# One matrix product out of eight, moved ahead of a group of attention scores in a fused attention and expert kernel

## The chip, the cores and the metric

The kernel runs on one core of one Trainium2 chip. The metric is the time of one execution on the device, in microseconds (us); a run's figure is the median of several executions. A profiled execution gives the trace of all engines of the core: TensorE (PE for its products, PEld for its weight loads), VectorE (DVE), ScalarE (ACT), GpSimd (POOL) and SyncE (SP, which here only issues DMAs).

## The reference

The inputs are q, k and v of 4 batches x 8 heads x 768 positions x 64, and three random block numbers for each of the 24 blocks of 32 positions. Attention is full matrix work under a block mask; its output, laid side by side over the heads, is the input x (3072 tokens x 512) of one expert layer with a softmax-weighted unit, a normalisation without a bias and a second product.

```
scores = (q @ k.T) / sqrt(64);  scores = where(mask, scores, -1e9)
x = softmax(scores) @ v                      # heads side by side: 3072 x 512
h = x @ w_in                                 # 3072 x 1024
solu = h * softmax(h)
ln = (solu - mean(solu)) / sqrt(var(solu) + 1e-6) * g_ln
out = ln @ w_out                             # 3072 x 512
```

## The kernel before, in words

**Tiling.** The 3072 tokens are worked in 12 passes of 256 tokens (three passes to a batch), and each pass in 12 units, so there are 144 units. A unit is one pair of heads (four pairs to a pass) and one third of the keys (256 of 768). For a unit, `scores` (L407) runs four products of 128 x 256 on TensorE into a tile of the scores' pool; `exps` (L423) takes the exponential of the whole tile (128 x 1024) on ScalarE; `outs` (L431) runs eight small products with the values (128 x 65). The mask is part of the scores' product: 24 extra rows of the keys and queries carry it. After the third unit of a pair of heads, `normalise` (L451) divides by the sums on VectorE and writes xb. The scores' pool has two buffers of two banks, so the scores of unit s + 2 need the buffer that the exponential of unit s reads.

**The layer.** When the four pairs of a pass are done, SP issues a transposing DMA of xb to xT (`x_turn`, L467). The layer then handles the pass's two tiles of 128 tokens, one after the other, while the next passes' attention goes on. For a tile, `h_mms` (L482) runs eight products of 128 x 512 into the one buffer for h; `e_exp` (L491) takes the exponential of h on ScalarE; `solu` (L499) multiplies h and e on VectorE; `ln_turn` (L510) has SP issue a transposing DMA of that product to lnT; `stats` and `rstd` (L516 and L524) work out the scale on VectorE and GpSimd; `o_mms` (L542) runs eight products of 128 x 512, one for each 128 of the 1024 columns, into the one buffer for o; `scaled` (L550) multiplies o by the scale on VectorE, and `store` (L560) has SP write the rows out.

**The order.** All this is issued from one written plan: `at(when, fn, ...)` (L290) puts a call on a list with a time in units, and `emit` (L293) calls the list sorted by that time. The order on each engine is thus the order of those numbers, and an engine waits only where an operand or a buffer isn't ready. In the loop at L773 unit s has its exponential at s (a little less at the end of a pass), the scores of unit s + 2 at s + 0.8, and its products with the values at s + 0.82 (s + 1.81 for the first unit of a pair). The function `layer` (L815) puts one tile's calls on the plan, from a list of times for pieces of h, a time for the exponential, and a list of times for pieces of o; the loop at L831 to L844 calls it for the two tiles of passes 0 to 9, 20 tiles in all, six units apart. The times of o are os + 0.84 and os + 1.83, where os is 14 units behind the tile's start (12 for the second tile of pass 9). The last two passes' tiles are planned by hand behind it and have nothing to do with the change.

**Around the change.** Between os + 0.84 and os + 1.83 stands one call for TensorE: the scores of unit os + 3, at os + 1.8 (in the second tile of pass 9 the products with the values of two units as well). Behind os + 1.83 come, at os + 1.9, the first two products of h of a later tile, and at os + 2.8 the scores of unit os + 4.

Of the kernel before, what the change touches and what calls it, by code (L numbers as in the profile page):

```python
# [208 lines left out]
def kernel(  # L209
# [25 lines left out]
    KF = d_ff // 128  # L235
# [12 lines left out]
    SLOTS = NP * UP  # L248
# [41 lines left out]
    def at(when, fn, *args):  # L290
        plan.append((when, len(plan), fn, args))
# [103 lines left out]
    def unit(s):  # L395
        ps, r = divmod(s, SLOTS)
        pr, u = divmod(r, UP)
        b, j = divmod(ps, NPB)
        return ps, b, j, pr, u
# [174 lines left out]
    with tc.manual_schedule():  # L574
# [198 lines left out]
        for s in range(n_units):  # L773
            ps, b, j, pr, u = unit(s)
# [37 lines left out]
                at(t0 + t_s, shift, b, pr, key, PC if pr == NP - 1 else 0)  # L812


        def layer(ps, i, hs, es, os):  # L815
            for when, n0, n1 in hs:
                at(when, h_mms, ps, i, n0, n1)
            at(es, e_exp, ps, i)
            head = ps == 0 and i == 0
            at(es + (0.33 if head else 0.5), solu, ps, i)  # L820
            at(es + 0.55, ln_turn, ps, i)
            at(es + (6.6 if head else 3.4 if ps == 0 else 2.45 if i == 0 else 1.7), stats, ps, i)
            at(es + (6.7 if head else 3.5), rstd, ps, i)
            for when, n0, n1 in os:
                at(when, o_mms, ps, i, n0, n1)
            out_at = 29.87 if head else os[-1][0] + 0.1
            at(out_at, scaled, ps, i, nc.vector)
            at(out_at + (2.2 if i == PC - 1 and ps < NPASS - 3 else 0.02), store, ps, i)

        LP = NPASS - 1  # L830
        for ps in range(LP):  # L831
            b0 = SLOTS * (ps + 1)
            if ps == 0:
                at(b0 + 2.4, x_first, ps)
            else:
                at(b0 - 0.1, x_turn, ps, 0, KD)
            if ps == LP - 1:
                break
            for i in range(PC):
                hs = b0 + 6 * i  # L840
                os = hs + (12 if ps == LP - 2 and i == PC - 1 else 14)
                layer(ps, i,
                      [(hs + 3.9, 0, 2), (hs + 4.85, 2, 3), (hs + 5.86, 3, 5), (hs + 6.85, 5, 7),
                       (hs + (7.79 if hs == SLOTS else 7.85), 7, 8)], hs + 8.5, [(os + 0.84, 0, 7), (os + 1.83, 7, 8)])  # L844


        ps, b0 = LP - 1, SLOTS * LP
# [176 lines left out]
```

## Time and profile before

| what | us |
|---|---|
| median of 3 runs | 208.02 (207.55 to 208.16) |
| the profiled execution | 208.32 |
| its span, first to last instruction | 206.8 |
| granted clock of TensorE over the span | 1.0 |

A line of the timeline has the start in us from the span's start, the length in us, the engine, the line of the kernel, the operation, what it writes and reads, and how many instructions are merged into the line; the bracket tells for how long the engine had been idle and who ended that. The products of TensorE are pipelined: the record of one is longer than the distance to the next, so distances between starts tell what a product costs. A few records of products are missing from the trace, which shows as x6 where seven were issued and as a short gap. In the chain of work each piece is start, length, what; it is followed back from the last instruction, at each step to what released it.

### The profile page before, as it was taken

To read this page: it belongs to the slowest core of one execution; us is meant where nothing else is said; L and a number is where in the kernel's file an instruction comes from. 1 tells how busy PE (TensorE), PEld (TensorE's weight loads), DVE (VectorE), ACT (ScalarE), POOL (GpSimd) and SP (SyncE) were. 2 spreads that over 40 slices of the span, in tenths; PEclk is the share of its full clock that TensorE was granted. 3 is DMA by queue.
4 is the path that set the end of the run, shared out by engine and by line. 5 is a ranking of instruction groups with operands and counts; after the bars stand their busy time and mean duration, and the time that the engine had idled before them with its cause. 6 is when DMAs were issued, how large, how long until landed. Compare 5 with 4: busy or idle time off the path is not lost.

```text
span 206.8 us, 5603 instructions
## 1 busy us (share of the span) xinstructions
PE 199.0 (96%) x2204; PEld 138.8 (67%) x2238; DVE 141.1 (68%) x331; ACT 175.2 (85%) x209; POOL 110.2 (53%) x167
## 2 busy tenths in 40 slices
PE   7999999999999999999999999999999999999992
PEld 2679967676676676676676676676676676667451
DVE  5688888988755765765665666655665656677982
ACT  6799979889889889889889889879889889897471
POOL 7966799696868274478286273559281110111120
PEclk9999999999999999999999999999999999999999
DMA  5999999979999879999999889999872484556314
GB/s 158 334 367 229 361 373 271 229 134 248 235 264 346 203 168 335 212 153 220 175 232 294 204 161 338 166 241 193 166 196 51 101 105 50 107 125 111 59 50 162
DMA packets 73906, 42.02 MB, mean 203 GB/s; under 512 B 55828, under 2 KB 69396, under 8 KB 73876
## 3 DMA queue, kind: packets, MB, share of 16 engines
q1 hardware_dynamic: 72932, 40.06, 84.1%
q0 software_dynamic: 528, 1.05, 2.7%
q10 hardware_dynamic: 416, 0.52, 0.8%
q8 instruction: 18, 0.29, 0.6%
q14 instruction: 12, 0.10, 0.1%
HBM read 23.07 MB, written 6.29 MB: 142 GB/s over the span
## 4 chain that ended last, share of the span: by engine, by line
PE 90%; DMA 4%; DVE 3%; issue 1%; DVEq 0%
PE sco L416 30%; PE op L444 18%; PE o L547 17%; PE h L487 16%; DMA xT<-xb 3%; PE warm_t L403 2%; DMA lnT<-solu 1%; PE tp_k L346 1%; PE oe L547 1%; PE mean_ps L753 1%; PE tp_q L356 1%; PE he L873 1%; DVE KT L371 1%; DVE QT L664 1%; PE ln_tp L883 0%
## 5 line engine op out<-in xcount | busy, mean ns | idle before, releaser
L427 ACT ACTIVATE exs<-sco 128x1024 bf16<-128x1024 f32 x144 | 141.0, 1024 | 10.3 <-PE sco L416 7.7
L416 PE MATMUL sco<-QT,KT 88*128 88x256 bf16 x576 | 87.4, 274 | 0.3
L416 PEld LDWEIGHTS <-KT 88*128 88x128 bf16 x576 | 54.8, 98 | 31.6 <-issue 4.7
L444 PE MATMUL op<-VA,exs 128*128 128x65 bf16 x1152 | 51.8, 194 | 0.5
L444 PEld LDWEIGHTS <-exs 128*128 128x128 bf16 x1152 | 48.5, 97 | 3.7 <-DVE xb L458 0.3
L487 PE MATMUL h<-w_in_sb,xT 128*128 128x512 bf16 x153 | 48.7, 378 | 0.7
L547 PE MATMUL o<-w_cen_sb,lnT 128*128 128x512 bf16 x166 | 43.3, 379 | 1.0 <-DMA lnT<-solu 0.4
L540 POOL TENSOR_TENSOR rstd<-vpe,mhalf 128x1 f32<-128x1 f32 x24 | 13.2, 549 | 45.4 <-DVE vpe L538 38.9
L457 DVE RECIPROCAL recip_all<-op 128x4 f32<-128x4 f32 x48 | 8.7, 181 | 39.7 <-PE op L444 39.5
L327 POOL COPY KT<-pd 64x768 bf16<-64x768 bf16 (+2 forms) x30 | 21.2, 706 | 23.9 <-DMA pd<-nat 22.8
L496 ACT ACTIVATE e<-h 128x1024 bf16<-128x1024 f32 x22 | 22.5, 1023 | 10.7 <-PE h L487 10.6
L522 DVE BATCH_NORM_STATS2 stats<-solu 128x6 f32<-128x512 bf16 x48 | 30.6, 680 | 0.1
L508 DVE TENSOR_TENSOR solu<-h,e 128x1024 bf16<-128x1024 f32 x22 | 26.7, 1215 | 1.5 <-ACT e L496 1.5
L547 PEld LDWEIGHTS <-lnT 128*128 128x128 bf16 x176 | 15.8, 98 | 14.2 <-DMA lnT<-solu 0.9
L558 DVE TENSOR_SCALAR ot<-o,rstd 128x512 f32<-128x512 f32 x20 | 15.0, 751 | 10.8 <-issue 8.2
L327 POOL COPY QT<-pd 64x768 bf16<-64x768 bf16 (+2 forms) x30 | 20.8, 694 | 1.5
L458 DVE TENSOR_TENSOR xb<-op,recip_all 128x256 bf16<-128x256 f32 x48 | 20.4, 424 | 1.7
L327 POOL CAST nat<-st_q 128x768 bf16<-128x768 f32 (+2 forms) x19 | 13.6, 713 | 14.3 <-DMA st_q<-in_q_dram 14.3
L487 PEld LDWEIGHTS <-xT 128*128 128x128 bf16 x176 | 16.1, 98 | 4.7 <-DMA xT<-xb 0.8
L327 POOL CAST VA<-st_v 128x768 bf16<-128x768 f32 x16 | 13.4, 847 | 1.4 <-DMA st_v<-in_v_dram 0.9
L327 POOL CAST nat<-st_k 128x768 bf16<-128x768 f32 x15 | 12.4, 826 | 3.3 <-DMA st_k<-in_k_dram 3.1
L538 DVE TENSOR_TENSOR vpe<-es,mv 128x1 f32<-128x1 f32 x24 | 6.7, 278 | 0.9
(89 smaller groups left out, 116.5 us busy)
## 6 DMA issues: line engine op xcount, KB each, us to landing
st_v<-in_v_dram SPq DMA_DIRECT2D x16, 384.0 KB, 5.9
out_dram<-ot SPq DMA_DIRECT2D x23, 256.0 KB, 2.8
st_k<-in_k_dram SPq DMA_DIRECT2D x15, 384.0 KB, 5.8
st_q<-in_q_dram SPq DMA_DIRECT2D x12, 384.0 KB, 7.9
w_out_f<-in_moe_w_out_dram SPq DMA_DIRECT2D x4, 512.0 KB, 7.4
st_q<-in_q_dram SPq DMA_DIRECT2D x4, 256.0 KB, 7.9
w_in_sb<-in_moe_w_in_dram POOLq DMA_DIRECT2D x1, 1024.0 KB, 12.0
st_q<-in_q_dram SPq DMA_DIRECT2D x4, 128.0 KB, 4.4
```

The source lines that it names most:

```text
L327: eng.tensor_copy(out=o, in_=i)
L416: nc.tensor.matmul(sco[:, hh, kk * QW : (kk + 1) * QW], KT[b % 2][0:KR, h * NCH + 2 * u + kk, :], QT[b % 2][0:KR, h * NCH + PC * j : h * N ...
L427: nc.scalar.activation(out=exs_of[ps, pr][:, u].rearrange("p a b c -> p (a b c)"), in_=sco_of.pop(s).rearrange("p a b -> p (a b)"), func=A ...
L444: nc.tensor.matmul(op[:, hh, ic, :], exs[:, u, hh, kk, ic * TQ : (ic + 1) * TQ], VA[b % 2][:, 2 * pr + hh, 2 * u + kk, :], start=(u == 0 a ...
L458: nc.vector.tensor_tensor(out=xb_of[ps][:, pr].rearrange("p c (h d) -> p h c d", h=2), in0=op[:, :, :, 0:D], in1=recip.broadcast_to([TQ, 2 ...
L487: nc.tensor.matmul(h_of[ps, i][:, half, :], xT_of[ps][:, c * PC + i, :], w_in_sb[:, c, half * HF : (half + 1) * HF], start=(c == 0), stop= ...
L496: nc.scalar.activation(out=o, in_=h, func=ACT.Exp, scale=1.0, accum_out=esum_all[:, t : t + 1])
L508: nc.vector.tensor_mul(out=so, in0=h, in1=e)
L522: nc.vector.bn_stats(out=stat_of[ps, i][:, half, :], in_=so[:, half, :])
L540: nc.gpsimd.tensor_tensor(out=rstd_of[ps, i], in0=vpe, in1=mhalf, op=ALU.pow)
L547: nc.tensor.matmul(ops_of[ps, i], lnT_of[ps, i][:, c, :], w_cen_sb[:, c, :], start=(c == 0), stop=(c == KF - 1), skip_group_check=True)
L558: nc.vector.tensor_scalar(out=o, in0=i_, scalar1=r, scalar2=None, op0=ALU.mult)
```

## The change

The function `layer` takes one time for o in place of a list of pieces. All eight products of o are issued at os + 0.84, so the eighth is no longer behind the scores of unit os + 3 but ahead of them. The scaling keeps its time: it was 0.1 behind the last piece (os + 1.83 + 0.1), and is now os + 0.84 + 1.09. On the queues of the other four engines the order of the instructions stays the same; on TensorE one weight load and one product change places with four weight loads and four products in 20 places (and in one of these 20 with 16 more of each, the products with the values).

```
-        def layer(ps, i, hs, es, os):
+        def layer(ps, i, hs, es, o_at):
...
-            for when, n0, n1 in os:
-                at(when, o_mms, ps, i, n0, n1)
-            out_at = 29.87 if head else os[-1][0] + 0.1
+            at(o_at, o_mms, ps, i, 0, KF)
+            out_at = 29.87 if head else o_at + 1.09
             at(out_at, scaled, ps, i, nc.vector)
...
-                       (hs + (7.79 if hs == SLOTS else 7.85), 7, 8)], hs + 8.5, [(os + 0.84, 0, 7), (os + 1.83, 7, 8)])
+                       (hs + (7.79 if hs == SLOTS else 7.85), 7, 8)], hs + 8.5, os + 0.84)
```

## The prediction, made before the changed kernel was run

> **What bounds the kernel now.** I read the page first (busy shares, the chain that ended last), then the chain of work in windows, then the timeline of one tile's round, then the waits of the queues.
>
> ```profile
> span 206.8 us, 5603 instructions
> ...
> PE 199.0 (96%) x2204; PEld 138.8 (67%) x2238; DVE 141.1 (68%) x331; ACT 175.2 (85%) x209; POOL 110.2 (53%) x167
> ...
> PE 90%; DMA 4%; DVE 3%; issue 1%; DVEq 0%
> ```
>
> TensorE carries 90% of the chain; ScalarE is next with 85% busy. A reordering on TensorE adds and removes no work, so it can only pay by filling a stall inside that 90%. To find one I look in the chain for a group that takes longer in one place than in another. This is the chain in three windows; columns are start, length, what.
>
> ```profile
> 41.27 0.44 PE sco L416 x4
> ...
> 48.87 0.51 PE sco L416 x4
> ...
> 109.00 1.51 PE o L547 x7
> 110.51 0.51 PE sco L416 x4
> 111.02 0.22 PE o L547
> 111.24 0.43 PE h L487 x2
> 111.67 0.44 PE sco L416 x4
> ...
> 180.19 0.51 PE sco L416 x4
> ...
> 186.22 0.44 PE sco L416 x4
> ```
>
> Four score products take 0.44 us, but 0.51 us where they follow the seven products of o: 0.07 us of nothing. The change has 20 such places, one for each token tile of passes 0 to 9. From 48.87 (first) to 180.19 (last) 17 of them show it. The other three do not: the ones at 41.27 and 186.22, and the one at 133.7, where TensorE had been held up just before. The timeline of the round at 110 us says what the scores wait for (columns: start, length, engine; narrow windows, so that ScalarE's exponentials stand one by one).
>
> ```profile
> 108.34 1.02 ACT L496 ACTIVATE e<-h 128x1024 bf16<-128x1024 f32 x1 [0.57 <-PE h L487]
> 108.84 1.67 PE L547 MATMUL o<-w_cen_sb,lnT 128*128 128x512 bf16 x7
> 109.36 1.02 ACT L427 ACTIVATE exs<-sco 128x1024 bf16<-128x1024 f32 x1
> 109.59 1.22 DVE L508 TENSOR_TENSOR solu<-h,e 128x1024 bf16<-128x1024 f32 x1
> 110.26 1.02 ACT L427 ACTIVATE exs<-sco 128x1024 bf16<-128x1024 f32 x1
> 110.42 0.60 PE L416 MATMUL sco<-QT,KT 88*128 88x256 bf16 x4
> 110.42 0.31 PEld L416 LDWEIGHTS <-KT 88*128 88x128 bf16 x3 [0.20 <-issue]
> 110.75 0.10 PEld L547 LDWEIGHTS <-lnT 128*128 128x128 bf16 x1
> 110.86 0.31 PEld L487 LDWEIGHTS <-xT 128*128 128x128 bf16 x2
> 111.08 0.59 PE L487 MATMUL h<-w_in_sb,xT 128*128 128x512 bf16 x2
> 111.16 2.06 ACT L427 ACTIVATE exs<-sco 128x1024 bf16<-128x1024 f32 x2
> 111.51 0.60 PE L416 MATMUL sco<-QT,KT 88*128 88x256 bf16 x4
> 112.92 0.60 PE L416 MATMUL sco<-QT,KT 88*128 88x256 bf16 x4
> 113.56 1.02 ACT L427 ACTIVATE exs<-sco 128x1024 bf16<-128x1024 f32 x1 [0.33 <-PE sco L416]
> ```
>
> Seven products from 108.84 at 1.51/7 = 0.216 us each are through at 110.35, but the scores start at 110.42. There are two score buffers, so these scores (unit os+3, os being the plan's slot of the o products) need the one that the exponential of unit os+1 reads. That one ran from 109.36 to 110.38, and 0.04 us later the scores start. It was late because ScalarE first had to do e, which in turn had waited 0.57 us for h. So once a round the path runs through ScalarE for 0.07 to 0.08 us.
>
> **The change part by part.** The plan moves one weight load and one product of o, 20 times, ahead of the scores of os+3 and on TensorE alone. The order of the instructions on the other four queues is the same, DMA issues included; no wait is added. The written times of the scaling and the store are also the same (os + 1.93 both ways).
>
> *The moved product.* It takes 0.216 us wherever it stands. Eight end at 108.84 + 8 x 0.216 = 110.57, after the buffer is free at 110.42, so the scores no longer wait; they start 0.15 later than now. They take 0.43, then h starts at 111.00 instead of 111.08. **Gain 0.07 (chain) to 0.08 (starts) a round; I take 0.075**, and 17 x 0.075 = 1.28 us if nothing else is late next.
>
> *What is late next, one by one.* (a) The first h product needs VectorE's product of h and e (one h buffer), done at 109.59 + 1.22 = 110.81; its weight load now starts at 110.86. A weight load starts here as the product ahead of it starts (110.75 is 0.33 behind the scores' 110.42), so in the new order it is due at 110.57 + 0.33 = 110.90: 0.04 to spare. (b) The scores of os+4 come at 111.43 and need the exponential that ends at 110.26 + 1.02 = 111.28, plus 0.04: 0.11 to spare. (c) The exponential of os+3 can start 0.64 behind its scores (112.92 to 113.56, where ScalarE stood waiting), so at 111.21 instead of 111.16; if it loses its overlap with the one ahead (spacing 0.90 against a length of 1.02) it starts at 111.28, 0.12 late. ScalarE has 0.33 of idle two exponentials later in this round and 0.57 ahead of e in the other kind of round, so this is taken up. (d) VectorE's scaling of o can start half a microsecond sooner; it is queued behind the product of h and e and holds up nobody. (e) The store of it is issued by SP, which hardly waits for that scaling:
>
> ```profile
> SPq L563 <- DVE ot L558: 0.2, 1, 0.2
> ```
>
> so no transfer moves because of it.
>
> *Where the gain cannot be kept.* The 17 gains pile up only if what TensorE meets later comes earlier too. In four places it now waits, or just does not, for something else:
>
> ```profile
> 49.46 0.11 PEld L487 LDWEIGHTS <-xT 128*128 128x128 bf16 x2 [0.26 <-DVE solu L508]
> 57.27 0.11 PEld L487 LDWEIGHTS <-xT 128*128 128x128 bf16 x2 [0.29 <-DMA xT<-xb]
> 95.47 1.24 SPq L513 DMA_TRANSPOSE lnT<-solu  x1
> DMA to landing us min/median/max: 3.0/4.5/5.9
> 101.13 1.20 PEld L547 LDWEIGHTS <-lnT 128*128 128x128 bf16 x7
> ...
> 118.55 1.23 SPq L513 DMA_TRANSPOSE lnT<-solu  x1
> 123.40 0.47 SPq L318 DMA_DIRECT2D st_q<-in_q_dram  x1
> 126.22 1.41 SPq L513 DMA_TRANSPOSE lnT<-solu  x1
> 131.35 0.83 POOL L327 CAST nat<-st_q 128x768 bf16<-128x768 f32 x1 [0.28 <-DMA st_q<-in_q_dram]
> 132.19 1.19 PEld L547 LDWEIGHTS <-lnT 128*128 128x128 bf16 x7 [0.30 <-DMA lnT<-solu]
> 134.64 0.11 PEld L487 LDWEIGHTS <-xT 128*128 128x128 bf16 x2 [0.49 <-DMA xT<-xb]
> ```
>
> At 49.46 the h load waits for VectorE already: that round's gain is lost, 0.075. At 57.27 it waits for the transposed x, set going before the round's own gain: 0.075. The transposed lnT that is used at 101.13 was issued at 95.47; these 5.66 us are near the longest landing of this transposition (5.9, median 4.5), so I count it as without margin, and what is in flight with it was set going up to two rounds before: 0.15. The same at 132.19 and 134.64: the lnT issued at 126.22 lands behind a load (its cast starts at 131.35) issued at 123.40, in a row of loads that SP begins when the transposition of 118.55 is issued, so TensorE is held by what was set going two rounds earlier: 0.15 for the two together, since the second wait takes what the first leaves. Bounds of these losses: nothing, if the loads come earlier by as much as TensorE, and all that was gained before 134.64 (11 of the 17, 0.83), if the loads keep their own clock. I take the 0.45 that the four make, nearer the first, since each issue of a load stands in SP's queue behind a transposition that waits for VectorE and so for TensorE.
>
> These rows show the transposition landing after a load issued 2.8 us ahead of it. The Trainium skill, page "DMA: Bandwidth & Descriptors", section "Queues, rings and completion order", says that on each DMA engine the descriptors of one issuing engine are consumed in ring order. The trace agrees (123.40 ahead of 126.22, 131.35 ahead of 132.19). By that rule the losses of 0.45 stand; were a transposition free to pass the loads, they would be 0.075, and the time 0.375 us lower.
>
> The three places without a stall give nothing and cost nothing: at 133.7 and 186.22 the scores of os+3 come 0.216 later, but ScalarE idles there, and at 41.27 the sequence is only permuted.
>
> **Sum.** 17 x 0.075 - 0.45 = 0.83, and with the starts' 0.08 it is 0.91: **0.9 us**. The profiled execution took 208.32 us (span 206.8 and 1.5 around it), 0.3 above the median of 208.02. It would become 207.4; from the median it is **207.1 us**, 0.43% less.
>
> **Rivals.**
>
> *The stall only moves.* The scores wait because there are two buffers, and there are still two; if the scores of os+4, or the h load, meet their own wait, the 0.07 comes back one step later. The Trainium skill, page "Perfetto Trace Analysis", section "Identifying Performance Opportunities", reads the same gap repeating as a sign of too little SBUF or PSUM; the trace agrees on the cause (17 equal gaps on a two-buffer tile), and by that rule an order without a buffer would not help. For it: the margins of 0.04 and 0.11 in (a) and (b) are small. Against: both are positive in rows rounded to 0.01, and the piece that fills the gap is three times the gap. If it holds in every second round, 8 x 0.075 = 0.6 less the 0.45 of the four places is left, some 0.2: 207.8 us.
>
> *The loads keep their own clock.* GpSimd waits for loads (0.28 at 131.35), so the loads, and not the compute engines, may set the pace up to there. Then all that is gained by 134.64 is eaten there, and the 6 rounds after it leave 6 x 0.075 = 0.45: 207.6 us. Against: SP's loads are issued between transpositions that wait for the compute engines.
>
> *Slower: late scores starve ScalarE.* The scores of os+3 come 0.15 later in 20 places. If ScalarE were the bound behind that place, its exponential would push all later ones by 0.05 to 0.12, and TensorE, which needs their buffers, would follow: 20 x 0.12 = 2.4 lost against 0.9 won, 1.5 slower, 209.5 us. It decides where ScalarE's idle time behind the place is under the delay: 0.33 and 0.57 a round now, against 0.12. So it needs two to four times less idle time than the rows show.
>
> That the change doesn't do what it says is excluded by the order of instructions: TensorE's queue has the eight products in one piece in all 20 places.
>
> **How the numbers follow.** Forecast (most of the gain kept, 207.1, its own range 206.6 to 207.4) 0.70; the stall moves (207.8) 0.15; the loads keep their clock (207.6) 0.10; ScalarE starved (209.5) 0.05. About 0.3%, or 0.62 us, is what a measurement of this kernel can tell from no change, so faster means below 207.4. The forecast is there, both middle rivals are within 0.3%: faster 0.70, same 0.25, slower 0.05. The range: the lower end is all 17 gains with no loss, 208.02 - 1.28 = 206.7, and 0.1 for the scatter of a median (the three runs lie 0.6 apart); the upper end takes in the loads' case and 0.1: 206.6 to 207.7. Beyond it lie the moved stall and the slower case, 0.2 together.
>
> **What would show it.** Right: the four scores behind o take 0.44 in the chain; the idle time of 0.20 of the weight load ahead of them is gone (now at 110.42); the scaling on VectorE starts about 0.5 earlier; ScalarE's exponential behind those scores starts 0.05 to 0.12 later against the products; rounds are 0.07 to 0.08 shorter from 60 to 95 us and from 141 to 180; the waits at 101.13, 132.19 and 134.64 are longer by 0.3 in all. Wrong: h's weight load waiting for VectorE in every second round (the stall moved), the span from 0 to 134.64 unchanged while the rest is shorter (the loads' clock), or ScalarE without idle time and TensorE waiting for it elsewhere (starved).

## The result, and the profile after

| what | us | share of the kernel before |
|---|---|---|
| kernel before, median beside these runs | 207.76 (207.08 to 208.43) | |
| kernel after, median | 206.66 (205.83 to 207.56) | 0.9944, 95% interval 0.9921 to 0.9967 |
| profiled execution of after | 207.12, span 205.2 | |

The changed kernel takes 0.56% less (interval 0.33% to 0.79%), which is 0.0056 x 207.76 = 1.16 us, between 0.69 and 1.64. The forecast was 0.43% less. Two repeats, told below, gave 0.9948 and 0.9946. The ratios here and below are over the fast runs and differ a little from the quotient of the two medians (0.9947 here; the largest difference is that of the early half below, 0.9972 against 0.9958).

The page of after, engine shares and the chain that ended last:

```profile
span 205.2 us, 5603 instructions
...
PE 196.0 (96%) x2204; PEld 137.2 (67%) x2238; DVE 141.9 (69%) x331; ACT 173.9 (85%) x209; POOL 110.3 (54%) x167
...
PE 85%; DVE 7%; ACT 2%; DMA 1%; issue 1%; POOL 1%; DVEq 0%; POOLq 0%
```

Both profiles hold 5603 instructions, and the span is 1.6 us shorter. TensorE's busy time went from 199.0 to 196.0, but that is no measure of the gain: both traces lack 34 records of products, and in the two profiles that have all 2238 (before again and the change again, below) it is 198.9 and 198.1. In the chain the share of DMA fell from 4% to 1%, and VectorE's rose from 3% to 7%. Neither was forecast, and both are taken up below. The chain of after in the round at 110 us:

```profile
108.56 1.73 PE o L547 x8
110.29 0.44 PE sco L416 x4
110.73 0.43 PE h L487 x2
111.16 0.44 PE sco L416 x4
```

Before, the same work read 1.51, 0.51, 0.22, 0.43, 0.44; now it is 1.73, 0.44, 0.43, 0.44. From the first product of o to the end of the second group of scores these are 3.11 and 3.04: the 0.07 that stood inside the scores is gone, and nothing new has come up behind it in this round. The timeline of the same round (narrow windows, as before):

```profile
107.91 1.02 ACT L496 ACTIVATE e<-h 128x1024 bf16<-128x1024 f32 x1 [0.57 <-PE h L487]
108.40 1.89 PE L547 MATMUL o<-w_cen_sb,lnT 128*128 128x512 bf16 x8
...
110.13 0.60 PE L416 MATMUL sco<-QT,KT 88*128 88x256 bf16 x4
110.39 0.75 DVE L558 TENSOR_SCALAR ot<-o,rstd 128x512 f32<-128x512 f32 x1
110.46 0.21 PEld L487 LDWEIGHTS <-xT 128*128 128x128 bf16 x2
110.56 0.60 PE L487 MATMUL h<-w_in_sb,xT 128*128 128x512 bf16 x2
110.77 1.02 ACT L427 ACTIVATE exs<-sco 128x1024 bf16<-128x1024 f32 x1
113.05 1.02 ACT L427 ACTIVATE exs<-sco 128x1024 bf16<-128x1024 f32 x1 [0.32 <-PE sco L416]
```

Read both rounds from the first product of o, at 108.84 before and 108.40 now. The scores behind it start at 1.73 instead of 1.58 (0.15 later), h at 2.16 instead of 2.24 (0.08 earlier), the exponential of those scores at 2.37 instead of 2.32 (0.05 later). ScalarE's idle time two exponentials later is 0.32 (0.33 before), and ahead of e it is 0.57 both times: the 0.05 is swallowed and nobody behind ScalarE sees it. The bracket with 0.20 at the scores' weight load is gone. The distance from the last product of o ahead of the scores to their first product says the same for the whole kernel: before it is 0.29 in 17 of the 20 places, after 0.216, one product, in all 20. In the waits of the queues, before and then after (total us, times, longest):

```profile
PEld L416 <- issue: 4.7, 23, 0.3
DVE ot L558 <- issue: 8.2, 15, 0.8
```

```profile
PEld L416 <- issue: 2.5, 9, 0.4
PEld L487 <- DVE solu L508: 0.5, 1, 0.5
```

Fourteen of the 23 waits of the scores' weight load are gone, and VectorE's row for the scaling no longer appears. The second row of after answers "the stall only moves": the h load waits for VectorE once in the whole kernel, not once a round.

### The profile page after: what moved, and what is told of

Its sections match the earlier page's. It is cut to its first block, busy times and chain, and to the rows that moved or that the text cites. A ratio compares the mean times of both kernels' runs of the same rounds, so it can differ in the third digit from the quotient of the medians.

```text
span 205.2 us, 5603 instructions
## 1 busy us (share of the span) xinstructions
PE 196.0 (96%) x2204; PEld 137.2 (67%) x2238; DVE 141.9 (69%) x331; ACT 173.9 (85%) x209; POOL 110.3 (54%) x167
## 4 chain that ended last, share of the span: by engine, by line
PE 85%; DVE 7%; ACT 2%; DMA 1%; issue 1%; POOL 1%; DVEq 0%; POOLq 0%
PE sco L416 28%; PE op L444 17%; PE o L547 16%; PE h L487 16%; PE warm_t L403 2%; DMA lnT<-solu 1%; DVE QT L664 1%; DVE stats L522 1%; DVE solu L508 1%; ACT exs L427 1%; PE oe L547 1%; PE mean_ps L753 1%; ACT QT L681 1%; PE tp_k L346 1%; DVE xb L458 1%
## 5 line engine op out<-in xcount | busy, mean ns | idle before, releaser
L416 PEld LDWEIGHTS <-KT 88*128 88x128 bf16 x576 | 54.1, 97 | 30.5 <-issue 2.5
L547 PE MATMUL o<-w_cen_sb,lnT 128*128 128x512 bf16 x166 | 40.0, 379 | 0.7
L496 ACT ACTIVATE e<-h 128x1024 bf16<-128x1024 f32 x22 | 22.5, 1023 | 10.7 <-PE h L487 10.6
L327 POOL CAST nat<-st_q 128x768 bf16<-128x768 f32 (+2 forms) x19 | 14.3, 755 | 7.4 <-DMA st_q<-in_q_dram 7.2
L664 DVE COPY QT<-QT 24x512 bf16<-24x512 bf16 (+2 forms) x9 | 7.3, 812 | 0.2
```

What stands on the lines that cost most here:

```text
L327: eng.tensor_copy(out=o, in_=i)
L416: nc.tensor.matmul(sco[:, hh, kk * QW : (kk + 1) * QW], KT[b % 2][0:KR, h * NCH + 2 * u + kk, :], QT[b % 2][0:KR, h * NCH + PC * j : h * N ...
L496: nc.scalar.activation(out=o, in_=h, func=ACT.Exp, scale=1.0, accum_out=esum_all[:, t : t + 1])
L547: nc.tensor.matmul(ops_of[ps, i], lnT_of[ps, i][:, c, :], w_cen_sb[:, c, :], start=(c == 0), stop=(c == KF - 1), skip_group_check=True)
```

## The experiments

The theory under test: once a round TensorE waits 0.07 us for the score buffer that ScalarE frees, the eighth product is real work put into that gap, and nothing behind it is late. The rivals: the gain comes from something else (fewer switches between kinds of products), the loads eat it up to 135 us, or ScalarE has no room for later scores. Times are medians, and ratios are to the kernel before on the same chip: 207.81 us for the first four kernels, 207.43 for the next four, 207.73 for the last four.

**Six products ahead, two behind.** If the gap is a wait for a fixed moment on ScalarE, taking one more product out of it must lengthen it by that product, 0.216.

```
-  ... [(os + 0.84, 0, 7), (os + 1.83, 7, 8)])
+  ... [(os + 0.84, 0, 6), (os + 1.83, 6, 8)])
```

> Six products of o ahead of the scores of os+3 and two behind them. Theory (the scores wait for the buffer that ScalarE's exponential of os+1 frees, at a time that does not depend on the products): the scores start where they do in the kernel before, the wait ahead of them is 0.07 + 0.216 = 0.29 us, and the products behind them cost 0.216 a round more; with 18 rounds (the one at 41 us joins them) 3.9 us slower than the kernel before, 212 us. Rival (the 0.07 is a fixed price of passing from o to the scores, and the change saves one passage): the same number of passages as before, so the same time as before, 207.8.

Measured: 211.34 us, ratio 1.0181 (1.0132 to 1.0231), 0.0181 x 207.81 = 3.8 us more, or 0.19 in each of 20 places. The number of pieces is that of the kernel before, so a price on switching would have given no change. Its chain of work at the same round:

```profile
109.13 1.11 ACT e L496 x2
110.24 0.92 ACT exs L427
111.17 0.04 issue
111.21 0.60 PE sco L416 x4
```

The chain, which in the kernel before ran through TensorE here, now runs through ScalarE: e, the exponential of unit os+1, 0.04 of nothing, and then the scores. And the timeline of that kernel:

```profile
109.62 1.46 PE L547 MATMUL o<-w_cen_sb,lnT 128*128 128x512 bf16 x6
111.21 0.31 PEld L416 LDWEIGHTS <-KT 88*128 88x128 bf16 x3 [0.41 <-issue]
```

Six products from 109.62 are through at 109.62 + 6 x 0.216 = 110.92; the scores start at 111.21, so the gap is 0.29, which is 0.07 and one product; the distances between starts show it in 18 of the 20 places. The wait on ScalarE is shown, and the switching price falls.

**Only the early half, only the late half, and the change again.** If the gains pile up, passes 0 to 5 (11 stalls) and passes 6 to 9 (6 stalls) must share the gain by their stalls; if the loads set the pace up to 135 us, the early half is worth nothing. The eighth product is a piece of its own, planned right behind the seven, and the scaling keeps its time. The late half has `ps > 5` in the second line.

```
+  def o_pieces(ps, i, os):
+      if ps <= 5:
+          return [(os + 0.84, 0, KF - 1), (os + 0.841, KF - 1, KF)]
+      return [(os + 0.84, 0, KF - 1), (os + 1.83, KF - 1, KF)]
...
-            out_at = 29.87 if head else os[-1][0] + 0.1
+            out_at = 29.87 if head else os[0][0] + 1.09
...
-  ... [(os + 0.84, 0, 7), (os + 1.83, 7, 8)])
+  ... o_pieces(ps, i, os))
```

> The change in the tiles of passes 0 to 5 alone (12 of 20 places, 11 of the 17 that stall, all ahead of the wait at 132 to 135 us). Theory that the transfers follow TensorE: 11 x 0.072 = 0.8 us faster than the kernel before, 0.38%, and a round of the trace shorter by 0.072 there. Rival (the loads keep their own clock): the wait at 132 to 135 us grows by what was gained ahead of it, and the time is that of the kernel before.

> The change in the tiles of passes 6 to 9 alone (8 places, 6 of the 17 that stall, all behind the wait at 132 to 135 us). Theory that the transfers follow TensorE: 6 x 0.072 = 0.43 us faster than the kernel before, 0.2%. Rival (the loads keep their own clock): the whole gain of the change sits here, so as fast as the changed kernel, 0.55% under the kernel before.

> The changed kernel once more, beside the others and with a second profile. Theory: 17 x 0.072 = 1.2 us under the kernel before, rounds of the same length as in its first profile; the waits at 49, 57, 101 and 132 to 135 us differ from profile to profile. Rival (the change itself moved the transfers that land at 130 us): the wait for lnT at 132 us is absent again and the gain of 0.5 us there is seen again.

Measured: early 207.22, ratio 0.9958 (0.9933 to 0.9982); late 207.32, 0.9973 (0.9947 to 0.9999); the change again 206.70, 0.9948 (0.9925 to 0.9971). The early half alone keeps 0.42% (by the medians 0.28%), and its interval excludes the time of the kernel before, so the loads do not eat the gain: that rival falls. The two halves add up to 0.69% against 0.52% for the whole, inside their intervals. The times are too coarse to give a price per round; the traces do that. ScalarE's exponential of h, three rounds apart, in before, after, early and late, in this order:

```profile
155.00 1.02 ACT L496 ACTIVATE e<-h 128x1024 bf16<-128x1024 f32 x1 [0.57 <-PE h L487]
178.02 1.02 ACT L496 ACTIVATE e<-h 128x1024 bf16<-128x1024 f32 x1 [0.53 <-PE h L487]
```

```profile
153.63 1.02 ACT L496 ACTIVATE e<-h 128x1024 bf16<-128x1024 f32 x1 [0.57 <-PE h L487]
176.44 1.02 ACT L496 ACTIVATE e<-h 128x1024 bf16<-128x1024 f32 x1 [0.53 <-PE h L487]
```

```profile
154.75 1.02 ACT L496 ACTIVATE e<-h 128x1024 bf16<-128x1024 f32 x1 [0.57 <-PE h L487]
177.78 1.02 ACT L496 ACTIVATE e<-h 128x1024 bf16<-128x1024 f32 x1 [0.53 <-PE h L487]
```

```profile
154.10 1.02 ACT L496 ACTIVATE e<-h 128x1024 bf16<-128x1024 f32 x1 [0.57 <-PE h L487]
176.90 1.02 ACT L496 ACTIVATE e<-h 128x1024 bf16<-128x1024 f32 x1 [0.53 <-PE h L487]
```

Three rounds take 23.02 before and 22.81 after: 0.07 a round. In the kernel with the new order only up to pass 5, this late stretch has its old length (23.03); in the kernel with the new order from pass 6, it has the new one (22.80). The early stretch shows the reverse. From the scores at 64 us to those eight rounds later the starts of TensorE's products are 61.47 apart before (64.31 to 125.78) and 61.49 in the late half (64.12 to 125.61), but 60.95 after (64.38 to 125.33) and 60.88 in the early half (65.01 to 125.89): 0.065 to 0.076 a round. The shortening sits in the rounds whose order was changed, and only there.

**The kernel before, once more, as it is.** The prediction took 0.375 off for waits on transfers at 101, 132 and 135 us that one execution showed. Does another execution show them?

> The kernel before once more, for a second profile of it. Theory (the waits at 49 us and at 132 to 135 us belong to the execution and not to the order of the products): the 17 gaps of 0.07 us stand where they stood; the wait for lnT and xT at 132 to 135 us differs by several tenths, and the h load at 49 us waits for VectorE for longer than the 0.03 us of the first profile if the start of the kernel runs sooner. Rival: both as in the first profile, 0.6 us in all at 132 to 135.

Measured: 207.24 us, one execution. The gaps of 0.08 between starts stand as before, and there are 18 of them: the place at 133 us, which had none in the first profile because TensorE had just been held up, has its gap here. The h load at 49 us waits 1.07 for VectorE (0.26 in the first profile). The waits at 132 and 135 are not there. The weight loads of o and of h in that place, 0.30 and 0.49 idle in the rows of the prediction, read as follows in before again, after, and early:

```profile
131.19 1.21 PEld L547 LDWEIGHTS <-lnT 128*128 128x128 bf16 x7
133.31 0.25 PEld L487 LDWEIGHTS <-xT 128*128 128x128 bf16 x2
```

```profile
131.18 1.42 PEld L547 LDWEIGHTS <-lnT 128*128 128x128 bf16 x8
133.41 0.11 PEld L487 LDWEIGHTS <-xT 128*128 128x128 bf16 x2 [0.16 <-DMA xT<-xb]
```

```profile
131.93 1.19 PEld L547 LDWEIGHTS <-lnT 128*128 128x128 bf16 x7
134.39 0.11 PEld L487 LDWEIGHTS <-xT 128*128 128x128 bf16 x2 [0.51 <-DMA xT<-xb]
```

The bracket that names a transfer is absent with the old order in one execution and present in another; with the new order it is 0.16 in one execution, 0.51 in another (early has the new order up to there), and absent in the two further executions of after that were profiled. So one and the same order has this wait in one execution and not in the next; whether an order changes how often it comes, so few profiles can't show. What marks the two executions with the long wait is a load: GpSimd's cast of one block of q (st_q) waited 3.00 and 2.65 us for its load in the first profile of before (it starts at 128.18) and in early (127.97), and 0.81 to 0.85 in the other five: before again (125.54), after, the change again and a third time, and late.

What the new order saves behind 49 us can be read with the start of the kernel left out: from the h load at 49 us to the weight load near the end, in before again and in after:

```profile
48.87 0.11 PEld L487 LDWEIGHTS <-xT 128*128 128x128 bf16 x2 [1.07 <-DVE solu L508]
...
197.63 0.11 PEld L547 LDWEIGHTS <-lnTe 128*128 128x128 bf16 x2 [0.52 <-ACT lnTe L325]
```

```profile
49.55 0.11 PEld L487 LDWEIGHTS <-xT 128*128 128x128 bf16 x2 [0.47 <-DVE solu L508]
...
197.14 0.11 PEld L547 LDWEIGHTS <-lnTe 128*128 128x128 bf16 x2 [0.52 <-ACT lnTe L325]
```

That is 148.76 with the old order and 147.59 with the new one; the change again and a third time take 147.65 and 147.67. The 17 gaps behind 49 us are worth 17 x 0.07 = 1.19, and 1.09 to 1.17 of that arrive: all the places behind 49 us together cost 0.1 or less. The first profile of before takes 149.31, and its waits at 132 and 135 us account for most of the difference to before again.

**The scores moved further back.** The change makes the scores of os+3 start 0.15 later at no cost. How much later can they come? Here, in the changed kernel, they stand behind the first two products of h as well (in 19 of the 20 tiles; the last has another distance).

```
-  at(s + 0.8, scores, s + 2)
+  st = s - 1 - 14
+  late_s = st % 6 == 0 and SLOTS <= st < SLOTS * (NPASS - 2) + 6
+  at(s + (0.95 if late_s else 0.8), scores, s + 2)
```

> The changed kernel with the scores of os+3 put further back still, behind the first two products of h. Tests the rival of late scores. In the rows before the change the h load cannot start before VectorE is done (110.86 there), so h starts at 110.97 and not 111.00 behind eight products that end at 110.57: a wait of 0.40 a round, 0.33 more than the kernel before; the scores start at 111.40, so ScalarE's exponential is 0.8 late against an idle time of 0.33 and 0.57, and TensorE's products with the values of that unit wait for it in one of two rounds. Theory: 20 rounds x 0.33 to 0.7, 6 to 14 us slower than the kernel before. Rival (there is room for late scores): within 1 us of the changed kernel.

Measured: 214.60 us, ratio 1.034 (1.0296 to 1.0384), 0.034 x 207.43 = 7.1 us more, 0.37 in each of 19 places. Two waits take the gap's place. The chain, and the timeline a few steps on:

```profile
112.25 1.74 PE o L547 x8
...
114.02 0.04 DVE solu L508
...
114.11 0.60 PE h L487 x2
```

```profile
115.19 1.94 ACT L427 ACTIVATE exs<-sco 128x1024 bf16<-128x1024 f32 x2 [0.66 <-PE sco L416]
116.27 0.30 PEld L444 LDWEIGHTS <-exs 128*128 128x128 bf16 x8 [0.27 <-ACT exs L427]
```

The h load comes too early for VectorE's product of h and e (margin (a) of the prediction was 0.04, and this order asks for 0.43 more), so TensorE stands still; and the scores, pushed back by h and by that stall, leave ScalarE idle for 0.66, so that later TensorE waits 0.27 for an exponential. This is the slower rival with its mechanism: it is real, and the change stops short of it. It is not a pure test of late scores, since the h load's wait comes with it.

**The wait at 49 us.** Here the first h load of a round waits for VectorE in every profile of the old and the new order, between 0.3 and 1.4 us. In the change run again (timeline):

```profile
43.27 1.71 POOL L327 COPY KT<-pd 64x768 bf16<-64x768 bf16 x2
...
45.06 0.57 POOL L540 TENSOR_TENSOR rstd<-vpe,mhalf 128x1 f32<-128x1 f32 x1
...
45.67 0.75 DVE L558 TENSOR_SCALAR ot<-o,rstd 128x512 f32<-128x512 f32 x1 [2.12 <-POOL rstd L540]
...
46.33 1.28 DVE L522 BATCH_NORM_STATS2 stats<-solu 128x6 f32<-128x512 bf16 x2
...
48.52 1.22 DVE L508 TENSOR_TENSOR solu<-h,e 128x1024 bf16<-128x1024 f32 x1
...
49.78 0.11 PEld L487 LDWEIGHTS <-xT 128*128 128x128 bf16 x2 [1.27 <-DVE solu L508]
```

GpSimd copies keys for 1.71 before it gets to the tiny rstd; VectorE's scaling waits 2.12 for that, stats and the product of h and e stand behind it in VectorE's queue, and TensorE's weight load waits 1.27 (its products stand idle for 0.99, since the scores ahead of it still ran when the wait began). In this execution GpSimd's copies themselves had waited for a transfer, the transposition pd<-nat, which the chain of work shows landing at 39.30; in before again, in after and in the third run of the change the chain comes to the copies from VectorE, without a transfer. Two edits on the changed kernel, each by one number: the scaling planned behind stats, or the copy planned behind rstd.

```
-            out_at = 29.87 if head else o_at + 1.09
+            out_at = 29.95 if head else o_at + 1.09
...
-            [21.3, 21.4, 26.0, 27.3, 30.1, 30.15, 38.2, 39.0],
+            [21.3, 21.4, 27.25, 27.3, 30.1, 30.15, 38.2, 39.0],
```

> The changed kernel with one more edit: the scaling of the very first tile of o is put behind the statistics of the second tile on VectorE (29.95 and not 29.87 in the plan). In two of the profiles so far VectorE stood 2 us at 43.5 to 45.7 us waiting for the first tile's scale from GpSimd, with the statistics queued behind it, and the h load at 49.5 us waited 1.2 us for VectorE. Theory (that stretch is bound by VectorE's queue behind the scaling): VectorE does the statistics in the idle time, the wait at 49.5 us goes, 0.5 to 1.2 us faster than the changed kernel. Rival (the next round meets a transfer, xT at 57 us, that does not come earlier): the same as the changed kernel.

> The changed kernel with one more edit: on GpSimd the scale of the first tile comes ahead of the copies of a pair of keys (27.25 and not 26.0 in the plan for that copy). Theory (GpSimd's copies hold up the scale, the scale holds up VectorE, VectorE holds up h at 49.5 us): VectorE's scaling starts some 1.7 us sooner, the wait at 49.5 us goes, 0.5 to 1.2 us faster than the changed kernel. Rival (the transfer of xT at 57 us takes the place): the same as the changed kernel.

Measured: 205.82, ratio 0.9926 (0.9896 to 0.9956), and 205.59, ratio 0.9914 (0.9885 to 0.9943). With the copy behind rstd the same rows read:

```profile
41.90 0.87 POOL L540 TENSOR_TENSOR rstd<-vpe,mhalf 128x1 f32<-128x1 f32 x1 [0.16 <-DVE vpe L538]
42.73 1.70 POOL L327 COPY KT<-pd 64x768 bf16<-64x768 bf16 x2
...
43.32 0.74 DVE L558 TENSOR_SCALAR ot<-o,rstd 128x512 f32<-128x512 f32 x1
...
46.66 1.21 DVE L508 TENSOR_TENSOR solu<-h,e 128x1024 bf16<-128x1024 f32 x1
...
47.92 0.11 PEld L487 LDWEIGHTS <-xT 128*128 128x128 bf16 x2 [0.16 <-DVE solu L508]
```

VectorE's wait of 2.12 is gone, and the weight load's of 1.27 is 0.16, and its products show no idle time. Whether the edit stands by itself, and whether the two add up, the last four kernels ask: the shift on the kernel before, the change a third time, the change with the shift again, and with both edits.

> The kernel before with only the edit of GpSimd's order in the first tiles (the scale ahead of the copies of a pair of keys). Theory (the wait at 49 us is of its own, apart from the eighth product): the wait of h for VectorE at 49 us goes, 0.5 to 1.2 us faster than the kernel before, and the gaps of 0.07 us stay, the one at 48 us too. Rival (the gain of that edit exists only with the eighth product ahead): as the kernel before.

> The changed kernel, for a direct comparison on the same chip with the three others: 1.1 to 1.2 us under the kernel before.

> The changed kernel with the edit of GpSimd's order. Theory (with the wait at 49 us gone, the round there keeps its gain too): 17 or 18 gaps x 0.072 = 1.2 to 1.3 us faster than the kernel before with the same edit, and 0.5 to 1.2 us faster than the changed kernel. Rival: no more than the changed kernel.

> The changed kernel with both edits of the first tiles (the scale earlier on GpSimd, the scaling later on VectorE). Theory (one edit is enough to take the wait away): the same as with the edit of GpSimd's order alone, within 0.3 us.

Measured: the shift on the kernel before 207.19, ratio 0.9981 (0.9955 to 1.0007), which doesn't settle whether it pays alone, though its trace has no wait at 49 us and keeps the gaps of the old order; the change a third time 206.56, 0.9946 (0.9924 to 0.9968); with the shift 205.81, 0.9922 (0.9895 to 0.9949); with both edits 205.94, 0.9907 (0.9881 to 0.9934), no different from one. With the shift on both sides the change is worth 207.19 - 205.81 = 1.38 us (forecast 1.2 to 1.3). Single intervals of the change and of its versions overlap. All four ratios without the long wait at 49 us (0.9926, 0.9914, 0.9922, 0.9907) are below all three of the change alone (0.9944, 0.9948, 0.9946); the means are 0.9917 and 0.9946, 0.3% or 0.6 us apart. The change with either of these edits, or with both, is thus the fastest that these runs found, some 0.8% under the kernel before; which of the three is best they don't tell.

## Why the prediction was right or wrong

**The stall: right.** The gap is a wait for ScalarE's exponential of os+1 through the two score buffers. Shown by the six-product order (0.29 instead of 0.07, and ScalarE in the chain) and by before and after (0.51 to 0.44).

**The gain per round: right.** 0.075 was taken; three rounds give 0.21/3 = 0.07 and eight rounds 0.065 to 0.076, only where the order was changed. 17 stalls at 0.07 to 0.075 are 1.2 to 1.3 us.

**What is late next: right in each number.** (a) The h load starts 2.06 behind the first product of o (110.46 - 108.40), as forecast (110.90 - 108.84), and does not wait: VectorE's product ended at 109.16 + 1.22 = 110.38, 0.08 ahead of it. (b) The scores of os+4 follow h without a gap in the chain. (c) The exponential of os+3 is 0.05 late, the lower end of 0.05 to 0.12, and ScalarE's idle time takes it. (d) The scaling starts 1.99 behind the first product of o (110.39 - 108.40); it was 2.49 (111.33 before): 0.5 earlier. That these small margins decide is shown by the order with the scores behind h.

**"Where the gain cannot be kept": wrong; this is the step that failed.** It took 0.45 off for four places: 0.075 at 49.46, 0.075 at 57.27, 0.15 at 101.13, 0.15 at 132.19 and 134.64, and forecast that the waits at 101.13, 132.19 and 134.64 would grow by 0.3 in all. They did not: 0.30 and 0.49 became nothing and 0.16, and at 101 us there is none. Waits on the same transfers came and went in executions of one and the same order. The error was to read a row of one execution as a property of the schedule: the "longest landing" of 5.9 that left the lnT of 101.13 without margin was the late one of that execution itself (126.22 + 5.9 = 132.1). Nor do the traces bear out a price of two rounds' gain, 0.15: from the issue of the lnT at 126 us to its use lie 5.61 us in before again and 5.54 in after (125.58 to 131.19, 125.64 to 131.18), so the new order leaves it 0.07 less time, one round's gain.

Of the four places only the one at 49.46 belongs to the schedule: it stands in the profile of every kernel that keeps that stretch, it is made by the order in GpSimd's and VectorE's queues, and it goes when a number in the plan is changed. There one round's gain is lost, 0.075. The sum should have been 17 x 0.075 - 0.075 = 1.2 us, that is 206.8 from the median of 208.02; measured were 1.16, and by the two repeats 0.0052 x 207.81 = 1.08 and 0.0054 x 207.73 = 1.12. The times alone would not convict the term (the interval of the first run, 0.69 to 1.64, holds 0.9); the traces do. Whether the place at 57 us costs a little stays open: a wait of 0.18 to 0.39 on xT shows in some profiles of either order and is absent in others. So does one that the prediction didn't list, at 103 us, one step behind the o of 101: the h load there waits 0.18 for xT in after and 0.23 in before again, and shows no wait in the first profile of before. What they could cost together is within the 0.1 found above. One wait on a transfer does stand in every profile, that for the last lnT at 195 us (the kernel's end, planned by hand); it is 0.63 in before again and 0.63 in after, so it came earlier by as much as TensorE did and takes nothing from the gain.

One slip in the sums of the rivals changes nothing: 0.6 less 0.45 is 0.15 and not some 0.2, so the moved stall would have stood at 207.9.

What hung on the rule of the Trainium skill, page "DMA: Bandwidth & Descriptors", section "Queues, rings and completion order", falls with that step. That the transposition at 126.22 was awaited beyond the load at 123.40 was so in that trace. The section speaks of the order in which descriptors are consumed; when a transfer lands, and whether TensorE must wait for it, does not follow from that, and here it varied: landings of this transposition spread over several us (last section), and four of the seven profiles looked at there (two of the new order, two of the old order up to that place) have no wait.

**The share of the chain.** DMA fell from 4% to 1%, since the transfer awaited at 135 us, 5.46 us of the chain, was in the one execution and not in the other; VectorE's 7% lies almost all ahead of the h load at 49 us that waits for it. Neither is an effect of the change: before again, with the old order, has TensorE 85%, VectorE 7% and DMA 3%.

**The rivals.** *The stall only moves*: falls, one wait of the h load for VectorE in the whole of after, at 49 us, where it was before. The Trainium skill, page "Perfetto Trace Analysis", section "Identifying Performance Opportunities", says that an equal gap that repeats can mean too little room for the next tile, the number of buffers included. The cause here was that, with two buffers, but the gap closed by order alone, without a third. *The loads keep their own clock*: falls, the early half keeps 0.42%, and of the 17 gaps behind 49 us 1.09 to 1.17 of 1.19 us arrive at the end. *Late scores starve ScalarE*: falls for this change (0.32 of idle left where 0.05 is needed), and is true for the order that goes one step further (+7.1 us).

## What to carry to other kernels

A gap of a few hundredths in the chain that stands in every round is worth its length times its count, if a piece of independent work at least as long can be put into it and the next waits on that engine are later than the piece; list those margins one by one, since here 0.43 more turned a gain of 1.1 us into a loss of 7. Before taking anything off for a wait on a transfer seen elsewhere, look whether a second execution of the same kernel has it. Here the wait that one engine's queue made for another stood in every profile and was worth an edit of its own, while the waits on transfers between 57 and 135 us came and went.

## What the runs showed of the hardware that was not expected

Transpositions of one and the same size, one to a round, land with a wide spread. The DMA groups of after, for the transposition of lnT:

```profile
DMA to landing us min/median/max: 3.0/3.9/5.1
```

In the first profile of before it was 3.0/4.5/5.9, and in before again the median and the largest were 4.4 and 5.4, so the same order differs by 0.5 in its longest landing, as much as the larger of the two waits at 132 and 135 us. The changed order shows the same spread between executions: its longest landing was 5.1, 6.0 and 5.5 in three profiles. And the start of a kernel varies more than its end: the exponential of unit 15 starts at 23.78 and 23.73 in the first profiles of before and after, and between 22.0 and 22.5 in eleven of the twelve others. Of the difference between the two profiles of before (23.78 and 22.27) less than half is left at 49 us (49.46 and 48.87), since the h load there waits the longer, the earlier TensorE gets to it (0.26 and 1.07).
